# Halving some key chunks on GpSimd, 24 instead of 60 identity products, and a newly searched instruction order in a fused attention and two-MLP kernel

## The chip, the cores and the metric

The kernel runs on one core of one Trainium2 chip. The metric is the device time of one execution in microseconds (us): 1506.7 us, the median of 3 runs (1506.11 to 1508.36). About 0.2%, some 3 us, is what a measurement of this kernel can tell from no change.

## What is computed

Three layers follow each other: an attention whose 768 keys are averages of 16 inputs each, an MLP with a squared ReLU, and an MLP with a rational activation. There are 12,288 tokens of 128 features; both MLPs have 2,048 hidden features.

```python
kv_pool = kv.reshape(B, H // r, r, W // r, r, C).mean(axis=(2, 4))   # r = 4: 16 inputs a key
k = v = kv_pool.reshape(B, -1, C) @ w_sr
s = scale * (q @ k.transpose(0, 2, 1)); a = softmax(s)
x = a @ v
r = np.maximum(x @ w_in, 0.0);  x = (r * r) @ w_out                  # first MLP
h = x @ w2_in
P = a[0] + a[1] * h + a[2] * h**2 + a[3] * h**3
Q = 1.0 + np.abs(b[0]) * np.abs(h) + np.abs(b[1]) * h**2
return (P / (Q + 1e-06)) @ w2_out                                    # second MLP
```

## The kernel before, in words

Tokens go through in 25 blocks: one of 384, 22 of 512, then 384 and 256. All activations lie features-first, so a product has 128 rows and up to 512 columns. To keep float32 accuracy, most products are split into a high and a low part and done as three fast (fp32r) products; the others are plain float32 products, which show as two instructions each. "room" is one large on-chip tensor: it first holds the 16 chunks of key inputs (48 keys of 16 inputs, 384 KB each) and afterwards, as numbered rings of buffers, the values between the stages (tags Z, U, K, g1, aT, e, o, qr).

At the start, `go2` (L480) sums the 16 inputs of each key on VectorE, chunk by chunk. Meanwhile TensorE multiplies an identity with itself (`warm`, L489, 60 times). `go` (L499) then makes the keys of one half from 8 chunks; ScalarE (L503) and VectorE (L507) split them into `k_hi` and `k_lo`; `decode` (L552 to L584) loads the MLP weights, which arrive as 64-bit numbers, and turns them into float32 with four VectorE operations a piece.

For each block there are then, by function:

- `attention`: scores (L671, 24 instructions a block), minimum (L675, VectorE), exponential (L678, ScalarE), the sum's reciprocal (L685, L686), scaling (L689, GpSimd), transposes (L712), their evacuation and split (L716 to L732, ScalarE or VectorE), the product with the values (L741 to L745), and the split of its result, `split` (L771 to L777).
- `mlp1`: `mm3` (L797 to L799) into a PSUM bank, ReLU (L839 on ScalarE or L842 on VectorE), square (L845 on ScalarE or L848 on GpSimd), for 10 of the 16 slices a split (L857, L863), and the output product `mmo` (L811 plain, L815 to L817 split).
- `mlp2`, in 8 groups of two slices: `mm3`; |h| (L936), a square of h (L950) and, for six groups, two GpSimd operations (L939, L941) or, for the other two, one on ScalarE (L944); a logarithm and an exponential (L961, L962); four VectorE operations (L952, L974, L976, L979); for two groups a split (L989 on ScalarE or L990 on VectorE, then L992 on GpSimd); the output product L811.

No loop sets the order in which these stand on each engine. `Plan.order` does, when the program is built: each piece of work is entered with a priority (`off` moves those of one kind), one or several engines it may run on with costs (`c_actp`, `c_dve2`, `c_pool` and so on) and a handicap for each (`rl_act`, `mh_dve`, ...), and the buffers and banks it needs (`bufs`, `caps`). The plan walks through time with these costs and writes out one fixed order for each engine. On the chip every engine takes its instructions strictly in that order. The table SQUARES holds the numbers for this branch of the program; a second table, TERMS, serves coefficients that the first form can't take, and doesn't run here.

Of the kernel before, what the change touches and what calls it, by code (L numbers as in the profile page):

```python
# [10 lines left out]
F32 = mybir.dt.float32  # L11
# [30 lines left out]
    lead1=17.5,  # L42
    leada=18.0,
# [2 lines left out]
    g=2,  # L46
    pair=('kk', 'qp', 'sq2', 'ln', 'y0', 'g0', 'tt', 'rr', 'g2', 'ml', 'mh'),
    rem=[],
    md_act=0.5,
    md_dve=0,  # L50
    rl_act=0,
    rl_dve=2,
    qh_act=0,
    qh_dve=8,
    spd=[],
    spl=[0, 3],
    qpool=[0, 1, 3, 4, 6, 7],
    sq_act=0,
    sq_pool=2,
    gh_act=0.5,  # L60
    gh_dve=60,
    mh_act=1,
    mh_dve=0.5,
    ml_pool=4,
    ml_dve=60,
    ev_dve=4,
    hi_dve=1,
    rg=1,
    low=5,
    avs=5,  # L70
    warm=60,
    head=[384],
    tail=[384, 256],
    off=dict(
        mh2=-197.25, mh1=-120.0, sc=0.25, tr=2.25, nr=-301.75, g2=-55.25, ex=-101.0, kk=-215.75, rl=-4.0,
        tt=68.25, ev=84.5, mo2=13.75, ln=84.25, g0=-20.75, ab=-96.25, sq=142.5, y0=36.0, mn=-267.75, qp=134.25,
        av=-195.25, mo1=5.5, sP=95.25, sq2=146.0, rr=248.75, mh=-48.5, ml=-221.5,
    ),
    free=150.0,
)  # L80
# [5 lines left out]
    lp=0,  # L86
# [282 lines left out]
def program(ctx, tc, CFG, fast, co, room, wsr, qT, kvT, w1_in, w1_out, w2_in, w2_out, outT):  # L369
# [32 lines left out]
    turn, ring_at, at = {}, {}, 0  # L402
    for t in [x for x in RINGS if x not in ("o", "qr")] + ["o", "qr"]:
        at = max(at, NKEY * R2) if t == "o" else at
        ring_at[t] = at
        at += RINGS[t] * bufs[t]
    assert at <= room_size(CFG)
# [46 lines left out]
    for t in RINGS:  # L454
        for n in range(bufs[t]):
            x = ring_at[t] + n * RINGS[t]
            P.hold[t, n] = [("poolT", c) for c in range(0, NKEY, KC) if c * R2 < x + RINGS[t] and x < (c + KC) * R2]
# [7 lines left out]
    def dma(prio, nbytes, emit, new=(), rd=(), wr=()):  # L465
        P.op(prio, (DMA, nbytes / 325.0 + 20.0, emit, 0), new, rd, wr)
# [6 lines left out]
        return go  # L473

    P.op(P0, (POOL, 500.0, lambda: make_identity(nc, ident), 0), new=[("const", "ident")])
    for c in range(0, NKEY, KC):
        def go2(c=c):
            t = mk("o", "pool") if c == 0 else tiles["pool"]
            kv = room[:, c * R2:(c + KC) * R2].rearrange("p (k r) -> p k r", r=R2)
            nc.vector.tensor_reduce(out=t[:, c:c + KC], in_=kv, axis=AX.X, op=ALU.add)  # L480
        dma(P0, KC * R2 * 512, lambda: None, new=[("const", ("kv", c))])
        P.op(P0, (DVE, c_dve(KC * R2), go2, 0), new=[("const", ("poolT", c))] + ([] if c else [("o", "pool")]),
             rd=[("kv", c)] + (["pool"] if c else []))
    dma(P0, sizes[0] * 512, load_q(0), new=[("qr", ("qr", 0))])

    def warm(i):
# [2 lines left out]
            nc.tensor.matmul(out=o[:, 0:128], lhsT=ident, rhs=ident, start=True, stop=True)  # L489
        return go  # L490
    for i in range(CFG["warm"]):
        P.op(1e6, (PE, c_mm4(128), warm(i), 0), new=[("st", "warm")] if i == 0 else [],
             rd=["ident"], wr=["warm"] if i else [])

    for h in range(2):
# [545 lines left out]
            emit()  # L1041


def room_size(cfg):

    n = {t: w * cfg["bufs"][t] for t, w in RINGS.items()}
    return max(sum(n.values()), 768 * 16 + n["o"] + n["qr"])


@with_exitstack  # L1050
def attn_moe_moe(
# [21 lines left out]
    room = pool.tile([128, max(room_size(SQUARES), room_size(TERMS))], F32, name="room")  # L1073
# [105 lines left out]
```

## Time and profile before

| | |
|---|---|
| median of 3 runs | 1506.7 us |
| the profiled execution | 1506.16 us |
| its span, first to last instruction | 1504.3 us |
| busy: TensorE (PE) | 1457.4 us, 97% |
| busy: ScalarE (ACT) | 1413.7 us, 94% |
| busy: VectorE (DVE) | 1388.8 us, 92% |
| busy: GpSimd (POOL) | 1314.7 us, 87% |
| chain that ended last | PE 64%, POOL 13%, ACT 12%, DVE 7%, issue 3% |

The profiled execution takes 1.9 us more than its span, and lies within the range of the runs. PE's busy time is modelled: products overlap in their pipeline, so the distance from one start to the next tells more than a product's duration. A wait is put down to the instruction whose semaphore came last.

### The profile page before, as it was taken

To read this page: it belongs to the slowest core of one execution; us is meant where nothing else is said; L and a number is where in the kernel's file an instruction comes from. 1 tells how busy PE (TensorE), PEld (TensorE's weight loads), DVE (VectorE), ACT (ScalarE), POOL (GpSimd) and SP (SyncE) were. 2 spreads that over 40 slices of the span, in tenths; PEclk is the share of its full clock that TensorE was granted. 3 is DMA by queue.
4 is the path that set the end of the run, shared out by engine and by line. 5 is a ranking of instruction groups with operands and counts; after the bars stand their busy time and mean duration, and the time that the engine had idled before them with its cause. 6 is when DMAs were issued, how large, how long until landed. Compare 5 with 4: busy or idle time off the path is not lost.

```text
span 1504.3 us, 18834 instructions
## 1 busy us (share of the span) xinstructions
PE 1457.4 (97%) x6063; PEld 1057.8 (70%) x6063; DVE 1388.8 (92%) x1848; ACT 1413.7 (94%) x2371; POOL 1314.7 (87%) x995
## 2 busy tenths in 40 slices
PE   6899999999999999999999999999999999999996
PEld 6777767766677677677676776777767667767764
DVE  6998999999999999999999998999988999999997
ACT  1789999999999999999999999999999999999997
POOL 1799998898998998988999889889889989899974
PEclk9999999999999999999999999999999999999998
DMA  7310000000000000000000000000000000000000
GB/s 266 112 50 7 6 8 15 8 8 15 7 8 8 15 4 11 8 8 15 8 8 15 8 8 7 15 8 7 15 7 8 8 11 6 8 5 4 7 8 12
DMA packets 15548, 28.62 MB, mean 19 GB/s; under 512 B 1744, under 2 KB 6736, under 8 KB 15440
## 3 DMA queue, kind: packets, MB, share of 16 engines
q1 hardware_dynamic: 15440, 27.34, 5.4%
q8 instruction: 49, 0.80, 0.2%
q14 instruction: 59, 0.48, 0.1%
HBM read 21.04 MB, written 6.29 MB: 18 GB/s over the span
## 4 chain that ended last, share of the span: by engine, by line
PE 64%; POOL 13%; ACT 12%; DVE 7%; issue 3%; DMA 0%; POOLq 0%; SPq 0%; ACTq 0%; DVEq 0%
PE psum L811 16%; PE psum L797 8%; PE psum L798 8%; PE psum L799 8%; PE psum L671 5%; POOL room L941 4%; PE psum L815 3%; PE psum L816 3%; PE psum L817 3%; PE psum L712 3%; POOL gL L863 2%; POOL room L939 2%; ACT room L950 2%; ACT room L961 2%; ACT room L936 2%
## 5 line engine op out<-in xcount | busy, mean ns | idle before, releaser
L941 POOL TENSOR_TENSOR room<-room 128x1024 f32<-128x1024 f32 (+2 forms) x150 | 347.3, 2316 | 3.0
L863 POOL TENSOR_TENSOR gL<-room,gH 128x512 fp32r<-128x512 f32 (+2 forms) x250 | 311.9, 1260 | 8.9 <-PE psum L816 2.6
L952 DVE SCALAR_TENSOR_TENSOR room<-room,cf,psum 128x512 f32<-128x512 f32 (+2 forms) x400 | 281.0, 719 | 16.5 <-ACT room L950 14.4
L811 PE MATMUL psum<-room,w1o 128*128 128x512 f32 (+2 forms) x600 | 288.8, 587 | 4.4 <-DVE room L979 4.4
L974 DVE SCALAR_TENSOR_TENSOR room<-room,v,psum 128x1024 f32<-128x1024 f32 (+2 forms) x200 | 246.3, 1233 | 29.7 <-ACT psum L962 27.8
L950 ACT ACTIVATE room<-psum,cf 128x512 f32<-128x512 f32 (+2 forms) x400 | 271.9, 709 | 0.0
L848 POOL TENSOR_TENSOR room<-room 128x512 f32<-128x512 f32 (+2 forms) x220 | 222.0, 1021 | 30.3 <-ACT room L839 19.0
L976 DVE SCALAR_TENSOR_TENSOR psum<-room,cf,psum 128x1024 f32<-128x1024 f32 (+2 forms) x200 | 247.3, 1237 | 0.0
L961 ACT ACTIVATE room<-room,cf 128x1024 f32<-128x1024 f32 (+2 forms) x200 | 229.2, 1148 | 17.9 <-POOL room L941 17.0
L979 DVE SCALAR_TENSOR_TENSOR room<-psum,room 128x1024 f32<-128x1024 f32 (+2 forms) x200 | 235.0, 1175 | 2.9
L936 ACT ACTIVATE room<-psum 128x512 f32<-128x512 f32 (+2 forms) x400 | 228.5, 608 | 6.1 <-PE psum L799 4.3
L939 POOL TENSOR_SCALAR room<-room,cf 128x1024 f32<-128x1024 f32 (+2 forms) x150 | 163.8, 1092 | 69.0 <-ACT room L936 57.2
L962 ACT ACTIVATE psum<-room 128x1024 f32<-128x1024 f32 (+2 forms) x200 | 206.0, 1031 | 4.1 <-DVE room L979 3.2
L797 PE MATMUL psum<-xh,w0h 128*128 128x512 f32 (+2 forms) x400 | 186.6, 466 | 4.2 <-ACT room L1012 1.5
L797 PE MATMUL psum<-yh,w1h 128*128 128x512 f32 (+2 forms) x400 | 185.5, 464 | 5.0 <-DVE room L952 1.3
L839 ACT ACTIVATE room<-psum 128x512 f32<-128x512 f32 (+2 forms) x272 | 161.6, 619 | 3.5 <-PE psum L799 3.1
L811 PEld LDWEIGHTS psum<-room,w1o 128*128 128x128 f32 x600 | 112.8, 193 | 66.5 <-issue 40.5
L857 ACT ACTIVATE gH<-room 128x512 fp32r<-128x512 f32 (+2 forms) x250 | 156.2, 659 | 0.7 <-POOL room L848 0.4
L799 PE MATMUL psum<-yh,w1l 128*128 128x512 f32 (+2 forms) x400 | 154.1, 385 | 0.0
L798 PE MATMUL psum<-yl,w1h 128*128 128x512 f32 (+2 forms) x400 | 153.8, 385 | 0.0
L798 PE MATMUL psum<-xl,w0h 128*128 128x512 f32 (+2 forms) x400 | 153.5, 384 | 0.2 <-DVE xl L777 0.2
L799 PE MATMUL psum<-xh,w0l 128*128 128x512 f32 (+2 forms) x400 | 153.5, 384 | 0.0
(126 smaller groups left out, 3196.4 us busy)
## 6 DMA issues: line engine op xcount, KB each, us to landing
room<-in_kv_dram SPq DMA_DIRECT2D x16, 384.0 KB, 7.8
room<-in_q_dram SPq DMA_DIRECT2D x22, 256.0 KB, 2.6
out_dram<-room SPq DMA_DIRECT2D x22, 256.0 KB, 2.0
room<-in_moe_w_in_dram SPq DMA_DIRECT2D x8, 512.0 KB, 3.9
room<-in_moe_w_out_dram SPq DMA_DIRECT2D x16, 256.0 KB, 2.7
room<-in_q_dram SPq DMA_DIRECT2D x2, 192.0 KB, 5.4
out_dram<-room SPq DMA_DIRECT2D x2, 192.0 KB, 1.9
room<-in_q_dram SPq DMA_DIRECT2D x1, 128.0 KB, 2.1
```

The source lines that it names most:

```text
L797: nc.tensor.matmul(out=out, lhsT=w_hi[m][:, sl], rhs=hi, start=True, stop=False)
L798: nc.tensor.matmul(out=out, lhsT=w_hi[m][:, sl], rhs=lo, start=False, stop=False)
L799: nc.tensor.matmul(out=out, lhsT=w_lo[m][:, sl], rhs=hi, start=False, stop=True)
L811: nc.tensor.matmul(out=o, lhsT=w_o[m][:, place[m][fi], :], rhs=rhs(), start=first, stop=last)
L863: nc.gpsimd.tensor_tensor(out=mk("gL", gl)[:, :T], in0=G(), in1=f(tiles[gh][:, :T]), op=ALU.subtract)
L936: one("ab", ACT, c_actp, lambda v: act(out=v(uu), in_=v(hh), func=AF.Abs), "U", [hh])
L941: one("qp", POOL, c_pool, lambda v: nc.gpsimd.tensor_tensor(out=v(ku), in0=v(ku), in1=v(uu), op=ALU.mult), None, [uu], [ku])
L950: one("sP", ACT, ptr(c_actp), lambda v: act(out=v(zz), in_=v(hh), func=AF.Square, bias=co["c"]), "Z", [hh])
L952: one("z3", DVE, ptr(c_dve), lambda v: stt(out=v(zz), in0=v(zz), scalar=co["nd"], in1=v(hh), op0=ALU.subtract, op1=ALU.mult), None, [hh], ...
L961: one("ln", ACT, ptr(c_acts), lambda v: act(out=v(uu), in_=v(ku), func=AF.Ln, bias=dl_ap), None, [ku], [uu])
L974: one("g0", DVE, ptr(c_dve), lambda v: stt(out=v(zz), in0=v(zz), scalar=e0, in1=v(yy), op0=ALU.add, op1=ALU.mult), None, [yy], [zz])
L976: one("tt", DVE, c_dl, lambda v: stt(out=v(yy), in0=v(ku), scalar=dl, in1=v(yy), op0=ALU.add, op1=ALU.mult), None, [ku], [yy])
```

## The change

Three things are done. On the 7 even chunks among the first 14, GpSimd adds the upper 8 inputs of each key to the lower 8 in place, and VectorE then sums 8 values instead of 16. The identity products go from 60 to 24. And nearly every number of the table SQUARES is new (handicaps, offsets, ring sizes, bank caps), as are some costs that the plan uses, so that the order on every engine is new from the start to the end. `places` also gives each ring buffer a place of its own, buffer by buffer, which says for which key chunk it must wait.

```diff
-    lp=1,
+    lp=0,
-        qr=1, qh=1, ql=1, e=4, mn=14, sm=16, aT=1, xh=1, xl=1, yh=2, yl=2, aH=2, aL=2, g1=8, U=2, K=4, Z=7, o=1,
+        qr=1, qh=1, ql=1, e=4, mn=17, sm=21, aT=1, xh=2, xl=1, yh=2, yl=2, aH=3, aL=2, g1=8, U=2, K=3, Z=7, o=1,
...
-        h2=3, yb=6, sc=6, st=6, x=1, h1=5, y1=1, y2=1, dc=1,
+        h2=6, yb=5, sc=6, st=6, x=1, h1=5, y1=1, y2=1, dc=1,
...
-    sq_act=0,
-    sq_pool=2,
+    sq_act=8,
+    sq_pool=0.5,
...
-    warm=60,
+    warm=24,
...
-    return (66 + n / 2) / 0.96 + 61 * ptr + 300
+    return (66 + n / 2) / 0.96 + 61 * ptr + 700
...
+    def half(c):
+
+        return c // KC % 2 == 0 and c < NKEY - 2 * KC
     for c in range(0, NKEY, KC):
         def go2(c=c):
             t = mk("o", "pool") if c == 0 else tiles["pool"]
             kv = room[:, c * R2:(c + KC) * R2].rearrange("p (k r) -> p k r", r=R2)
+            if half(c):
+                kv = kv[:, :, 0:R2 // 2]
             nc.vector.tensor_reduce(out=t[:, c:c + KC], in_=kv, axis=AX.X, op=ALU.add)
...
+        def add2(c=c):
+            kv = room[:, c * R2:(c + KC) * R2].rearrange("p (k r) -> p k r", r=R2)
+            nc.gpsimd.tensor_tensor(out=kv[:, :, 0:R2 // 2], in0=kv[:, :, 0:R2 // 2], in1=kv[:, :, R2 // 2:], op=ALU.add)
...
+        if half(c):
+            P.op(P0, (POOL, c_pool(KC * R2 // 2), add2, 0), wr=[("kv", c)])
...
```

Counted over the whole executed branch, the new order moves these between engines (instructions before, after). Squares: ScalarE 180, 139 (L845), GpSimd 220, 261 (L848). ReLUs: ScalarE 272, 255 (L839), VectorE 128, 145 (L842). High parts of the second MLP: ScalarE 32, 26 (L989), VectorE 18, 24 (L990). Low parts in the attention: GpSimd 25, 0 (L728), VectorE 100, 125 (L732), and 25 copies that fed the GpSimd form (L716, L719) are gone. New: 7 additions on GpSimd. TensorE does the same work but for 36 identity products.

The new file is longer: what stood at L489, L499, L507, L566 stands at L497, L507, L515, L574 now, and L848, L863, L939, L941 are L856, L871, L947, L949.

The first place is the start on TensorE, from the identity products (L489, then L497) to the first scores. Before:

```order
L489 MATMUL psum<-ident 128x128 x57
L499 MATMUL psum<-room,wsr 128x384
L514 MATMUL psum<-wsr,room 128x128 x3
L489 MATMUL psum<-ident 128x128 x3
L499 MATMUL psum<-room,wsr 128x384
L514 MATMUL psum<-wsr,room 128x128 x3
L671 MATMUL psum<-k_hi,qh 128x384 x2
```

In the changed kernel:

```order
L497 MATMUL psum<-ident 128x128 x24
L507 MATMUL psum<-room,wsr 128x384
L522 MATMUL psum<-wsr,room 128x128 x3
L507 MATMUL psum<-room,wsr 128x384
L522 MATMUL psum<-wsr,room 128x128 x3
L679 MATMUL psum<-k_hi,qh 128x384 x2
```

The first key product stood behind 57 identity products and stands behind 24 now; the second has none ahead of it any more.

The second place is the same stretch on VectorE, from the sums of the key inputs (L480, then L482) to the low part of the second half of the keys (the second L507, then L515). Before:

```order
L480 TENSOR_REDUCE room<-room 128x48 x10
L507 SCALAR_TENSOR_TENSOR k_lo<-psum,k_hi 128x384
L480 TENSOR_REDUCE room<-room 128x48
L529 SCALAR_TENSOR_TENSOR v_lo<-psum,v_hi 128x384
L480 TENSOR_REDUCE room<-room 128x48 x5
L566 TENSOR_SCALAR psum<-room 128x512
L574 SCALAR_TENSOR_TENSOR psum<-room,psum 128x512
L507 SCALAR_TENSOR_TENSOR k_lo<-psum,k_hi 128x384
```

In the changed kernel:

```order
L482 TENSOR_REDUCE room<-room 128x48 x12
L515 SCALAR_TENSOR_TENSOR k_lo<-psum,k_hi 128x384
L482 TENSOR_REDUCE room<-room 128x48 x4
L537 SCALAR_TENSOR_TENSOR v_lo<-psum,v_hi 128x384
L574 TENSOR_SCALAR psum<-room 128x512
L582 SCALAR_TENSOR_TENSOR psum<-room,psum 128x512
L587 SCALAR_TENSOR_TENSOR psum<-room,psum 128x512
L515 SCALAR_TENSOR_TENSOR k_lo<-psum,k_hi 128x384
```

Two more sums stand ahead of the first low part, and three weight operations instead of two ahead of the second.

The third place is GpSimd in the middle of the run, from the low part of one block's queries (ql, the 13th) on. Before:

```order
L650 TENSOR_TENSOR ql<-room,qh 128x512
L689 TENSOR_SCALAR room<-room,sm 128x768
L863 TENSOR_TENSOR gL<-room,gH 128x512
L939 TENSOR_SCALAR room<-room,cf 128x1024
L848 TENSOR_TENSOR room<-room 128x512
L728 TENSOR_TENSOR aL<-room,aH 128x512
L941 TENSOR_TENSOR room<-room 128x1024
L863 TENSOR_TENSOR gL<-room,gH 128x512 x3
```

In the changed kernel:

```order
L658 TENSOR_TENSOR ql<-room,qh 128x512
L697 TENSOR_SCALAR room<-room,sm 128x768
L856 TENSOR_TENSOR room<-room 128x512
L697 TENSOR_SCALAR room<-room,sm 128x768
L856 TENSOR_TENSOR room<-room 128x512
L947 TENSOR_SCALAR room<-room,cf 128x1024
L856 TENSOR_TENSOR room<-room 128x512
L949 TENSOR_TENSOR room<-room 128x1024
```

The attention's low part (L728) is gone from the queue, and three squares (L856) stand where one stood, two of them ahead of the first of the second MLP's products (L947) and one between it and its second half (L949).

## Rows read from the trace of the kernel before

**Rows 1.** The page: busy time of each engine over the whole span.

```profile
PE 1457.4 (97%) x6063; PEld 1057.8 (70%) x6063; DVE 1388.8 (92%) x1848; ACT 1413.7 (94%) x2371; POOL 1314.7 (87%) x995
```

**Rows 2.** Busy time by stretch: us, each engine's busy us (instructions), granted clock, DMA.

```profile
50.00:100.00 50.00, 49.05 (x259) 42.41 (x258) 48.16 (x106) 44.97 (x99) 45.02 (x48) 1.00 0.33 105
60.00:1440.00 1380.00, 1368.69 (x5629) 985.40 (x5628) 1289.83 (x1661) 1339.79 (x2219) 1261.66 (x942) 1.00 0.04 12
1450.00:1500.00 50.00, 38.59 (x148) 27.09 (x146) 45.14 (x70) 41.08 (x85) 26.34 (x23) 0.83 0.02 5
```

**Rows 3.** Timeline of the start: start us, length us, instruction, idle time before it.

```profile
8.13 14.77 PE L489 MATMUL psum<-ident 128*128 128x128 f32 x114 [8.13 <-POOL ident masks.py:199]
9.20 8.69 DVE L480 TENSOR_REDUCE room<-room 128x48 f32<-128x768 f32 x10 [0.65 <-DVE cf L1089]
...
22.73 0.81 PE L499 MATMUL psum<-room,wsr 128*128 128x384 f32 x2
...
24.17 0.56 DVE L507 SCALAR_TENSOR_TENSOR k_lo<-psum,k_hi 128x384 fp32r<-128x384 f32 x1 [6.28 <-ACT k_hi L503]
...
30.40 1.65 PE L499 MATMUL psum<-room,wsr 128*128 128x384 f32 x2 [5.52 <-DVE room L480]
...
32.61 0.56 DVE L507 SCALAR_TENSOR_TENSOR k_lo<-psum,k_hi 128x384 fp32r<-128x384 f32 x1 [0.93 <-ACT k_hi L503]
```

**Rows 4.** Line L1083, the 16 loads of key inputs: first and last issue, landing.

```profile
L1083 SPq DMA_DIRECT2D room<-in_kv_dram x16: 327/416/646, 2.1 to 14.0; - x16
...
DMA to landing us min/median/max: 4.6/7.8/8.2
```

**Rows 5.** Timeline, issue of the first weight loads on the DMA queue.

```profile
16.01 2.27 SPq L552 DMA_DIRECT2D room<-in_moe_w_in_dram  x3
```

**Rows 6.** Busy time by stretch around the second key product, granted clock after the engines.

```profile
28.00:30.00 2.00, 0.00 (x0) 0.00 (x0) 2.00 (x3) 0.00 (x0) 0.03 (x1) 0.74 1.04 336
32.00:34.00 2.00, 2.00 (x10) 2.00 (x9) 1.21 (x3) 1.04 (x3) 0.00 (x0) 0.50 0.15 52
```

**Rows 7.** Timeline of the DMA queue: two of the blocks' stores, 17 blocks apart.

```profile
225.53 0.34 SPq L1016 DMA_DIRECT2D out_dram<-room  x1
...
1239.68 0.34 SPq L1016 DMA_DIRECT2D out_dram<-room  x1
```

**Rows 8.** The chain that ended last: start us, length us, what; PE's pace.

```profile
654.89 1.41 PE psum L671 x8
656.30 0.23 PE psum L797
...
659.03 0.23 PE psum L815
...
661.93 3.43 PE psum L811 x8
...
801.80 1.21 PE psum L712 x11
```

**Rows 9.** Groups by line and shape: count, busy us, mean ns, idle before.

```profile
L848 POOL TENSOR_TENSOR room<-room 128x512 f32<-128x512 f32 x196 | 204.2, 1055 | 27.4 <-ACT room L839 17.2 <-DVE room L842 4.7 <-DVE sm L685 2.5
...
L845 ACT ACTIVATE room<-room 128x512 f32<-128x512 f32 x156 | 99.0, 664 | 0.9 <-DVE room L842 0.6
...
L732 DVE TENSOR_TENSOR aL<-psum,aH 128x512 fp32r<-128x512 f32 x88 | 59.5, 684 | 2.3 <-ACT aH L722 1.7
...
L989 ACT ACTIVATE mH<-room 128x1024 fp32r<-128x1024 f32 x27 | 29.5, 1092 | 0.0
...
L728 POOL TENSOR_TENSOR aL<-room,aH 128x512 fp32r<-128x512 f32 x22 | 28.3, 1288 | 0.5
...
L990 DVE CAST mH<-room 128x1024 fp32r<-128x1024 f32 x17 | 23.9, 1406 | 0.8 <-PE psum L817 0.6
```

**Rows 10.** Waits, 60 to 1440 us: total us, times, longest us.

```profile
PE psum L797 <- ACT room L678: 2.5, 4, 1.3
...
ACT room L961 <- POOL room L941: 13.5, 32, 1.2
```

More of the change, by code (lines that the diff above doesn't have):

```diff
@@ L48 @@
     rem=[],
-    md_act=0.5,
-    md_dve=0,
-    rl_act=0,
+    md_act=1,
+    md_dve=60,
+    rl_act=8,
     rl_dve=2,
-    qh_act=0,
-    qh_dve=8,
+    qh_act=4,
+    qh_dve=1,
     spd=[],
     spl=[0, 3],
-    qpool=[0, 1, 3, 4, 6, 7],
-    sq_act=0,
-    sq_pool=2,
+    qpool=[0, 1, 3, 4, 5, 7],
+    sq_act=8,
+    sq_pool=0.5,
     gh_act=0.5,
     gh_dve=60,
-    mh_act=1,
-    mh_dve=0.5,
-    ml_pool=4,
+    mh_act=8,
+    mh_dve=0,
+    ml_pool=0,
     ml_dve=60,
-    ev_dve=4,
-    hi_dve=1,
+    ev_dve=8,
+    hi_dve=0,
     rg=1,
-    low=5,
+    low=4,
     avs=5,
-    warm=60,
+    warm=24,
     head=[384],
@@ L400, in program @@
     tiles = {}
[L402 to L407, printed above, removed]
+    turn = {}
+    place_of, extra = places(CFG, None if fast else room_size(SQUARES))
+    more = const.tile([128, extra], F32, name="more") if extra else None
     def mk(tag, key, shape=None, dtype=None):
@@ L414, in mk @@
             n = turn[tag] = turn.get(tag, -1) + 1
-            at = ring_at[tag] + n % bufs[tag] * RINGS[tag]
-            t = room[:, at:at + RINGS[tag]]
+            in_room, at = place_of[tag, n % bufs[tag]]
+            t = (room if in_room else more)[:, at:at + RINGS[tag]]
             if dtype:
@@ L453, in program @@
     P = Plan(CFG)
[L454 to L457, printed above, removed]
+    for (t, n), (in_room, x) in place_of.items():
+        P.hold[t, n] = [("poolT", c) for c in range(0, NKEY, KC)
+                        if in_room and c * R2 < x + RINGS[t] and x < (c + KC) * R2]
     def f(t):
@@ L479, in go2 @@
             kv = room[:, c * R2:(c + KC) * R2].rearrange("p (k r) -> p k r", r=R2)
+            if half(c):
+                kv = kv[:, :, 0:R2 // 2]
             nc.vector.tensor_reduce(out=t[:, c:c + KC], in_=kv, axis=AX.X, op=ALU.add)
-        dma(P0, KC * R2 * 512, lambda: None, new=[("const", ("kv", c))])
-        P.op(P0, (DVE, c_dve(KC * R2), go2, 0), new=[("const", ("poolT", c))] + ([] if c else [("o", "pool")]),
-             rd=[("kv", c)] + (["pool"] if c else []))
+        def add2(c=c):
+            kv = room[:, c * R2:(c + KC) * R2].rearrange("p (k r) -> p k r", r=R2)
+            nc.gpsimd.tensor_tensor(out=kv[:, :, 0:R2 // 2], in0=kv[:, :, 0:R2 // 2], in1=kv[:, :, R2 // 2:], op=ALU.add)
+        P.op(P0, (DMA, KC * R2 * 512 / 520.0, lambda: None, 0), new=[("const", ("kv", c))])
+        if half(c):
+            P.op(P0, (POOL, c_pool(KC * R2 // 2), add2, 0), wr=[("kv", c)])
+        P.op(P0, (DVE, c_dve(KC * R2 // (2 if half(c) else 1)), go2, 0),
+             new=[("const", ("poolT", c))] + ([] if c else [("o", "pool")]), rd=[("kv", c)] + (["pool"] if c else []))
     dma(P0, sizes[0] * 512, load_q(0), new=[("qr", ("qr", 0))])
@@ L491, in program @@
     for i in range(CFG["warm"]):
-        P.op(1e6, (PE, c_mm4(128), warm(i), 0), new=[("st", "warm")] if i == 0 else [],
+        P.op(1e6, (PE, 260.0, warm(i), 0), new=[("st", "warm")] if i == 0 else [],
              rd=["ident"], wr=["warm"] if i else [])
@@ L1041, in program, with places @@
             emit()
+def places(cfg, size):
+    bufs, at, out = cfg["bufs"], 768 * 16, {}
+    for t in ("o", "qr"):
+        for n in range(bufs[t]):
+            out[t, n] = (True, at)
+            at += RINGS[t]
+    low, extra = 0, 0
+    for t in RINGS:
+        for n in range(0 if t in ("o", "qr") else bufs[t]):
+            w = RINGS[t]
+            if low + w <= 768 * 16:
+                out[t, n], low = (True, low), low + w
+            elif size is None or at + w <= size:
+                out[t, n], at = (True, at), at + w
+            else:
+                out[t, n], extra = (False, extra), extra + w
+    return (out, extra) if size is not None else (out, 0)
 def room_size(cfg):
-    n = {t: w * cfg["bufs"][t] for t, w in RINGS.items()}
-    return max(sum(n.values()), 768 * 16 + n["o"] + n["qr"])
+    return max(x + RINGS[t] for (t, n), (_, x) in places(cfg, None)[0].items())
 @with_exitstack
@@ L1072, in attn_moe_moe @@
     wsr = pool.tile([128, w_sr.shape[1]], F32, name="wsr")
[L1073 removed]
+    room = pool.tile([128, room_size(SQUARES)], F32, name="room")
     col = lambda n, name: pool.tile([128, n], F32, name=name)
```

12 lines of the change are left out of this document (6 added, 6 removed).

## The prediction

> **What bounds the kernel now.** I read the page first: TensorE is busy 97% of the span, ScalarE 94%, VectorE 92%, GpSimd 87% [rows 1]. Four nearly full engines say little by a mean, so I cut the run into start, middle and end. In the middle, 1380 us, ScalarE is busy for 1339.8 us (97.1%), VectorE for 93.5%, GpSimd for 91.4%; in the 50 us before the end TensorE is busy for 38.6 us only, VectorE for 45.1 us [rows 2].
>
> How much TensorE waits in the middle is seen in its pace. Two stores 17 blocks apart give (1239.68 - 225.53) / 17 = 59.66 us a block [rows 7]. Where TensorE runs without a gap, 12 fp32r products of 512 columns take 2.73 us (0.2275 each), 8 score products 1.41 us (0.176), 8 halves of plain products 3.43 us (0.857 a whole one), 11 transposes 1.21 us (0.11) [rows 8]. A block has 153, 24, 19 and 24 of them: 34.8 + 4.2 + 16.3 + 2.6 = 57.9 us. So TensorE is the bound, and 59.66 - 57.9 = 1.76 us a block is lost waiting, some 40 us over the 23 blocks of the middle. No order can save more than that there.
>
> In the start I read the timeline. The identity products run from 8.13 us; the first key product starts at 22.73 us, directly behind them [rows 3]. Its data was there sooner: VectorE did 10 sums in 8.69 us from 9.20 us on, so the eighth was done at 16.2 us. VectorE then had a low part (L507) next, which needs that key product, and sat idle 6.28 us for it until 24.17 us with six sums still to do. So the second key product waited for the last sum until 30.40 us [rows 3]. The identity products thus held up VectorE, and VectorE the keys.
>
> **The start, step by step.** Removing 36 of 60 identity products: at the mean pace of the 57 that stood first, (22.73 - 8.13) / 57 = 0.256 us, 24 end near 14.3 us, before the eighth sum. The first key product then goes at about 16.3 us, and the idle 6.28 us are gone. What is late next is the data: the 16 chunk loads are issued until 14.0 us and land 7.8 us later, 8.2 at most [rows 4]. The last chunk is there at about 22 us, its full sum (8.69 / 10 = 0.87 us) ends at 23.0. The second key product moves from 30.40 to about 23.0: 7.4 us.
>
> Not all of it arrives at the scores. Behind the sums VectorE now has three weight operations, not two, ahead of the second low part. They need the first weights, issued at 16.01 us [rows 5] behind the key chunks, and so hardly there before 24 to 25 us. I have no row for one of them alone; a sum of 768 inputs at 0.87 us is the nearest long one, and 0.684 us for a 512-wide VectorE operation [rows 9] is the nearest in size. I take the latter: 25.2 + 3 x 0.684 = 27.3 us, so the low part is at 27.3 us where it was at 32.61 [rows 3]. I take **5.5 us** as gained. The ends are 0 (the lead is lost again until about 60 us, as the weights arrive no sooner) and 8 (all of it stays, and the shorter sums help).
>
> The 7 additions on GpSimd: a GpSimd operation of 512 pairs takes 1.055 us [rows 9], one of 384 is bounded by that and by 384/512 of it, 0.79. There is one addition for every two chunks, and chunks are issued 11.9 / 15 = 0.79 us apart [rows 4], so GpSimd, which has no other work there, keeps up. They spare VectorE at most 7 x 0.87 / 2 = 3.0 us of sums. As the data sets the end of the sums, I cost and credit them nothing; without that cover the range of the term holds them.
>
> Fewer identity products also mean a cooler start. After its idle time the clock fell: 0.74 at 28 to 30 us, 0.50 (1.2 GHz) at 32 to 34 us [rows 6]. With the key products at 16.3 and 23.0 us the idle time between is about 5.5 us, as long as now, so I expect the same fall 7 us earlier, and no cost. If the low clock lasted 4 us of TensorE work longer, that would cost 2 us; the range of the term holds it.
>
> **The middle, step by step.** ScalarE loses 36 full-width squares at 0.664 us (23.9 us) and 5 high parts at 1.092 us (5.5 us) [rows 9]. Its other full-width forms net to two instructions less (1.3 us), and narrower ones take off perhaps 4 us: **35 us** less. GpSimd takes the 36 squares at 1.055 us (+38.0) and drops 22 low parts at 1.288 us (-28.3) [rows 9]: 10 us more. VectorE takes 5 high parts at 1.406 us (+7.0), and its 0.684 us forms net to two more (L732 +22, L842 +12, L725 -16, L719 -11, L774 -5) [rows 9]: about 9 us more.
>
> So ScalarE's idle time in the middle goes from 40 to some 75 us, GpSimd's from 118 to 108, VectorE's from 90 to 81 [rows 2]. What TensorE waits for there is small in each place. The view of its waits lists 15 pairs with 11.3 us in all, the largest on the exponential L678 with 2.5 us [rows 10]; the pairs that end on ScalarE make 6.0 us of it, just over half. I charge half of the 40 us lost to ScalarE and let it shrink as ScalarE's idle time grows, 20 x (1 - 40/75) = 9 us. The other half grows with the lost idle time of the two others, about a tenth of 20, so 2 us, which leaves a gain of 7. A regular order can give a little more, since what is lost are short waits in places that the new order treats anew; I take **8 us**. Ends: all 40 us gained, which no row supports with three engines above 90%, and a loss, the rival below.
>
> **The end** has the same VectorE operations on its last two blocks, in nearly the same order, and VectorE is its busiest engine [rows 2]. I cost it at 0, with 2 us either way.
>
> **The sum.** Against the profiled execution, 1506.16 us (0.5 us under the median of the runs): 1506.2 - 5.5 - 8 = **1492.7 us**.
>
> A rule against the change: the Trainium skill, in GPSIMD Engine Reference, section 4.1, advises VectorE and not GpSimd for elementwise products, since two-input operations run about twice as long there. The same square indeed takes 1.055 us on GpSimd and 0.664 us on ScalarE here [rows 9]. By the rule the moved squares are a bad trade, and the sum would be that of the slower rival below; by the rows they buy time on the fuller engine.
>
> **Rivals.**
>
> *Only the start gains.* TensorE's 1.76 us a block comes from bursts, in which the order of a few instructions matters and not an engine's mean. Then a lighter ScalarE changes nothing: 1506.2 - 5.5 = 1500.7 us. For it: no single wait of TensorE's is long [rows 10]. Against it: ScalarE has only 40 us idle in 1380.
>
> *The middle gains much more.* Half of the 40 us go, as all four queues get shorter: 1506.2 - 5.5 - 20 = 1480.7 us. For it: the order is new everywhere. Against it: VectorE and GpSimd get more work.
>
> *Nothing is left.* The start's lead is lost while the weights are loaded, since VectorE is busy for 48.2 of the 50 us after 50 us [rows 2], and the middle stays: 1506 us.
>
> *Slower, by GpSimd's queue.* The added squares stand between the two GpSimd operations of the second MLP (L939, L941), and ScalarE's logarithm waits for L941 already, 32 times, 13.5 us in all, up to 1.2 us [rows 10]. If a square delays that chain as far as TensorE, it costs its 1.055 us; all 41 would cost 43 us. Without a gain in the middle, slower by over 0.2% is reached when a fifth of them do, (5.5 + 3) / 43. With 27% it is 11.6 us: 1506.2 - 5.5 + 11.6 = 1512.3 us. Against it: GpSimd has 118 us idle in the middle, and lost 22 longer operations from its queue.
>
> That the change doesn't do what it says is excluded by the order: 24 identity products, 7 additions and 41 squares moved all stand there.
>
> **How the numbers follow.** The forecast gets 0.45 (its own range 1485 to 1499), only the start 0.17, the large gain 0.15, nothing left 0.12, slower 0.11. About 0.2%, 3 us, is what a measurement can tell from no change. Faster by more: 0.45 + 0.17 + 0.15 = 0.77; within it 0.12; slower 0.11. The range 1479 to 1507 takes in the first four cases nearly whole and leaves out the slower one and the outer part of the large gain, under 0.2.
>
> **What would show it.** In the new profile the first key product should start near 16 us and the second near 23 us, with no idle time of 6 us on VectorE between. ScalarE's busy time should be about 35 us lower, GpSimd's 10 to 17 higher. The distance of 17 stores should give 59.2 to 59.5 us a block. I am wrong if the second key product moves and the scores do not, if the blocks stay at 59.66 us, or if TensorE's waits now end on GpSimd lines.

## The result, and the profile after

The changed kernel takes 1487.57 us (median of 4 runs, 1486.91 to 1488.9) against 1507.48 us for the kernel before beside it: a ratio of 0.987, 95% interval 0.9853 to 0.9887, so 19.6 us less. It lies in the range given, on the side given most, and 5 us under the predicted 1492.7 us. The profiled execution takes 1486.91 us, its span 1484.7 us where 1504.3 us stood.

Busy times on the page of the changed kernel:

```profile
PE 1439.5 (97%) x5991; PEld 1053.8 (71%) x5991; DVE 1386.9 (93%) x1857; ACT 1393.4 (94%) x2318; POOL 1334.1 (90%) x1021
```

Against [rows 1], ScalarE is 20.3 us less busy (35 were expected), GpSimd 19.4 more (10 to 17), VectorE 1.9 less (9 more). ScalarE and GpSimd moved the way that was forecast, by other amounts; VectorE moved the other way.

The start in the timeline of the changed kernel, TensorE and VectorE (start us, length us, instruction, idle time before it):

```profile
8.23 7.63 PE L497 MATMUL psum<-ident 128*128 128x128 f32 x48 [8.23 <-POOL ident masks.py:199]
...
10.01 5.50 DVE L482 TENSOR_REDUCE room<-room 128x48 f32<-128x384 f32 x8 [0.68 <-issue]
...
15.69 0.81 PE L507 MATMUL psum<-room,wsr 128*128 128x384 f32 x2
...
19.95 3.13 DVE L482 TENSOR_REDUCE room<-room 128x48 f32<-128x768 f32 x4
...
23.14 1.65 PE L507 MATMUL psum<-room,wsr 128*128 128x384 f32 x2 [5.97 <-DVE room L482]
23.70 0.70 DVE L574 TENSOR_SCALAR psum<-room 128x512 int32<-128x512 int32 x1 [0.16 <-DMA room<-in_moe_w_in_dram]
...
25.72 0.78 PE L679 MATMUL psum<-k_hi,qh 128*128 128x384 f32 x2
25.77 0.55 DVE L515 SCALAR_TENSOR_TENSOR k_lo<-psum,k_hi 128x384 fp32r<-128x384 f32 x1
```

The key products start at 15.69 and 23.14 us (forecast 16.3 and 23.0), the second low part at 25.77 us where it was at 32.61 [rows 3]: 6.8 us sooner, not 5.3 (27.3). The step that was too long is the wait for the first weights: they were there at 23.70 us, not 25.2. VectorE's idle time of 6.28 us is gone; TensorE's stop ahead of the second key product, 5.97 us, stays, as forecast. So does the clock's fall:

```profile
22.00:24.00 2.00, 0.86 (x2) 0.56 (x3) 1.84 (x4) 0.74 (x2) 0.97 (x1) 0.50 1.01 401
...
26.00:28.00 2.00, 2.00 (x13) 1.98 (x12) 2.00 (x5) 1.55 (x4) 0.00 (x0) 0.97 0.96 321
```

These are windows of the changed kernel, the granted clock behind the engines' busy times: 0.50 (1.2 GHz) at 22 to 24 us, after TensorE had stood for 5.97 us, and 0.97 in the window 4 us on. As before, a second fall follows it.

In the middle, busy time of the changed kernel from 60 to 1420 us:

```profile
60.00:1420.00 1360.00, 1351.47 (x5579) 981.80 (x5579) 1279.40 (x1648) 1311.95 (x2150) 1262.61 (x945) 1.00 0.03 11
```

and of the kernel before:

```profile
60.00:1420.00 1360.00, 1348.69 (x5539) 971.38 (x5538) 1270.68 (x1639) 1320.34 (x2179) 1242.37 (x922) 1.00 0.04 12
```

In the same 1360 us TensorE starts 40 more products. At 1351.47 / 5579 = 0.242 us each that is 10 us of work, an estimate, as products differ in length. The first 60 us, before:

```profile
0.00:60.00 60.00, 40.72 (x239) 37.77 (x240) 45.16 (x108) 22.40 (x48) 19.15 (x25) 0.91 0.55 193
```

and in the changed kernel:

```profile
0.00:60.00 60.00, 40.61 (x212) 36.03 (x213) 51.34 (x127) 30.07 (x65) 33.75 (x42) 0.89 0.64 222
```

Without the identity products (120 and 48 instructions) these are 119 and 164, so the changed kernel is 45 products ahead at 60 us and 85 at 1420 us. By the same 0.242 us the 85 are 20.6 us, as much as the whole gain: the end adds nothing that this estimate can tell. The second key product starts 7.3 us sooner, so some 12 of the 19.6 us are gained in the middle.

The stores, which were to show the pace, mislead:

```profile
237.88 0.34 SPq L1024 DMA_DIRECT2D out_dram<-room  x1
...
1213.73 0.34 SPq L1024 DMA_DIRECT2D out_dram<-room  x1
```

(1213.73 - 237.88) / 17 = 57.40 us a block where [rows 7] gave 59.66, less even than the 57.9 us of TensorE's unbroken work in the prediction. The new order finishes blocks at other points of its run; the distance of two stores is no pace then.

Waits, 60 to 1420 us (total us, times, longest us), of the kernel before: ScalarE's longest, then three of TensorE's, PEld being the weight load ahead of a product:

```profile
ACT room L961 <- POOL room L941: 12.9, 31, 1.2
...
PEld psum L797 <- DVE room L952: 14.0, 35, 1.2
PEld psum L797 <- ACT room L839: 12.6, 28, 1.3
PEld psum L797 <- ACT room L678: 8.7, 14, 1.8
```

and of the changed kernel, with the largest wait of a product itself (PE) as the last:

```profile
ACT room L969 <- POOL room L949: 20.8, 38, 1.7
...
PEld psum L805 <- DVE room L960: 11.2, 32, 1.2
...
PEld psum L805 <- ACT room L686: 5.3, 8, 1.2
...
PEld psum L805 <- ACT room L847: 3.5, 12, 0.4
...
PE psum L824 <- POOL mL L1000: 1.8, 4, 0.8
```

Summed over all of the view's pairs, products and loads that wait for ScalarE go from 42.8 to 22.7 us, for VectorE from 54.6 to 48.3, for GpSimd from 13.0 to 10.1. (Loads run ahead of products, so these us are not all lost; they show where TensorE is held.) The prediction would have been wrong if TensorE's waits now ended on GpSimd: the largest wait of a product does (L1000, 1.8 us), but GpSimd's sum is still the smallest of the three. The logarithm's wait for GpSimd grew from 12.9 us to 20.8, as the slower rival had it. TensorE's loads (L797, now L805) don't wait longer for the last VectorE operation behind that chain: 6.1 us for L979 before, 4.7 for L987 now.

### The profile page after: what moved, and what is told of

It is laid out like the page before. It is cut to its first block, busy times and chain, and to the rows that moved or that the text cites. A ratio compares the mean times of both kernels' runs of the same rounds, so it can differ in the third digit from the quotient of the medians.

```text
span 1484.7 us, 18746 instructions
## 1 busy us (share of the span) xinstructions
PE 1439.5 (97%) x5991; PEld 1053.8 (71%) x5991; DVE 1386.9 (93%) x1857; ACT 1393.4 (94%) x2318; POOL 1334.1 (90%) x1021
## 4 chain that ended last, share of the span: by engine, by line
PE 67%; POOL 13%; ACT 8%; DVE 7%; issue 3%; DMA 1%; SPq 0%; POOLq 0%; ACTq 0%; DVEq 0%
PE psum L819 17%; PE psum L805 9%; PE psum L806 8%; PE psum L807 8%; PE psum L679 4%; PE psum L824 4%; POOL room L949 4%; PE psum L825 4%; PE psum L823 4%; PE psum L720 4%; POOL gL L871 3%; POOL room L947 2%; POOL room L856 2%; PE psum L750 1%; PE psum L749 1%
## 5 line engine op out<-in xcount | busy, mean ns | idle before, releaser
L949 POOL TENSOR_TENSOR room<-room 128x1024 f32<-128x1024 f32 (+2 forms) x150 | 348.3, 2322 | 3.6
L871 POOL TENSOR_TENSOR gL<-room,gH 128x512 fp32r<-128x512 f32 (+2 forms) x250 | 313.0, 1262 | 20.8 <-PE psum L824 15.8
L819 PE MATMUL psum<-room,w1o 128*128 128x512 f32 (+2 forms) x600 | 285.2, 583 | 4.0 <-DVE room L987 4.0
L856 POOL TENSOR_TENSOR room<-room 128x512 f32<-128x512 f32 (+2 forms) x261 | 262.3, 1022 | 12.5 <-ACT room L847 6.6
L982 DVE SCALAR_TENSOR_TENSOR room<-room,v,psum 128x1024 f32<-128x1024 f32 (+2 forms) x200 | 246.1, 1232 | 21.2 <-ACT psum L970 19.4
L958 ACT ACTIVATE room<-psum,cf 128x512 f32<-128x512 f32 (+2 forms) x400 | 262.8, 688 | 0.0
L987 DVE SCALAR_TENSOR_TENSOR room<-psum,room 128x1024 f32<-128x1024 f32 (+2 forms) x200 | 235.2, 1177 | 3.1
L944 ACT ACTIVATE room<-psum 128x512 f32<-128x512 f32 (+2 forms) x400 | 223.4, 593 | 12.5 <-PE psum L807 6.5
L947 POOL TENSOR_SCALAR room<-room,cf 128x1024 f32<-128x1024 f32 (+2 forms) x150 | 164.7, 1098 | 48.3 <-ACT room L944 36.0
L970 ACT ACTIVATE psum<-room 128x1024 f32<-128x1024 f32 (+2 forms) x200 | 202.7, 1015 | 0.7 <-DVE room L960 0.3
L805 PE MATMUL psum<-yh,w1h 128*128 128x512 f32 (+2 forms) x400 | 191.2, 478 | 4.8 <-DVE room L987 3.5
L805 PE MATMUL psum<-xh,w0h 128*128 128x512 f32 (+2 forms) x400 | 182.8, 457 | 1.6 <-DVE xh L782 1.2
L847 ACT ACTIVATE room<-psum 128x512 f32<-128x512 f32 (+2 forms) x255 | 148.3, 601 | 5.1 <-PE psum L807 3.2
L865 ACT ACTIVATE gH<-room 128x512 fp32r<-128x512 f32 (+2 forms) x250 | 149.8, 632 | 2.9 <-POOL room L856 2.6
```

What stands on the lines that cost most here:

```text
L805: nc.tensor.matmul(out=out, lhsT=w_hi[m][:, sl], rhs=hi, start=True, stop=False)
L819: nc.tensor.matmul(out=o, lhsT=w_o[m][:, place[m][fi], :], rhs=rhs(), start=first, stop=last)
L856: nc.gpsimd.tensor_tensor(out=G(), in0=G(), in1=G(), op=ALU.mult)
L871: nc.gpsimd.tensor_tensor(out=mk("gL", gl)[:, :T], in0=G(), in1=f(tiles[gh][:, :T]), op=ALU.subtract)
L949: one("qp", POOL, c_pool, lambda v: nc.gpsimd.tensor_tensor(out=v(ku), in0=v(ku), in1=v(uu), op=ALU.mult), None, [uu], [ku])
L958: one("sP", ACT, ptr(c_actp), lambda v: act(out=v(zz), in_=v(hh), func=AF.Square, bias=co["c"]), "Z", [hh])
```

## The experiments

Two theories stood at first. **Load:** the middle gains since work left ScalarE, the fullest helper. **Order:** it gains since the order searched happens to have fewer places where TensorE is held, whatever the engines' loads. Differences from the kernel before are (ratio - 1) x 1507.5 us, each against runs of the kernel before beside it; the intervals are about 2.5 us either way (1.5 us for a3, b1 and n1, with more runs).

### The start: identity products, additions

Two edits of the kernel before keep its order. The first issues 24 of 60 identity products; the second adds the additions and half sums to that:

```diff
+            if i < 24:
                 nc.tensor.matmul(out=o[:, 0:128], lhsT=ident, rhs=ident, start=True, stop=True)
```
```diff
             kv = room[:, c * R2:(c + KC) * R2].rearrange("p (k r) -> p k r", r=R2)
+            if c // KC % 2 == 0 and c < NKEY - 2 * KC:
+                nc.gpsimd.tensor_tensor(out=kv[:, :, 0:R2 // 2], in0=kv[:, :, 0:R2 // 2], in1=kv[:, :, R2 // 2:], op=ALU.add)
+                kv = kv[:, :, 0:R2 // 2]
```

Two edits of the changed kernel undo parts and keep the new order: full sums without additions (the addition's line is taken out too), and, beyond that, 60 identity products, all of them ahead of the first key product.

```diff
-            if half(c):
-                kv = kv[:, :, 0:R2 // 2]
```
```diff
+            for _ in range(37 if i == 0 else 1):
                 nc.tensor.matmul(out=o[:, 0:128], lhsT=ident, rhs=ident, start=True, stop=True)
```

> The kernel before with its own order, in which only the first 24 of the 60 identity products are issued. Theory (the start's gain is the identity products alone and lasts to the end): the second key product moves from 30.4 us to about 23.5 us and the time falls by 6 to 8 us against before. Rival (the start's lead is lost again while the weights are loaded): the key product moves and the time stays within 1.5 us of before.

> As the run with 24 identity products, with the seven GpSimd additions and the shorter sums on VectorE as well, order otherwise that of before. Theory (the last chunk's arrival ends the sums): within 1 us of the run with 24 identity products alone. Rival (VectorE's sums end the start): 2 to 3 us faster than that run.

> The changed kernel with its order, without the seven additions, so that VectorE sums all 16 inputs of every key. Theory (arrival ends the sums): 0 to 1 us slower than the changed kernel. Rival (the additions carry part of the gain): 2 to 4 us slower.

> The changed kernel's order with the old start: 60 identity products ahead of the first key product and no additions, so only the new order from there on is left of the change. Theory (start about 7 us, middle about 12): 5 to 7 us slower than the changed kernel, some 13 us faster than before. Rival (all of the gain is the middle): within 1.5 us of the changed kernel.

| run | us | ratio (95%) | against before |
|---|---|---|---|
| before, 24 identity products | 1500.99 | 0.9953 (0.9937 to 0.997) | -7.1 |
| the same, with additions | 1499.84 | 0.995 (0.9934 to 0.9967) | -7.5 |
| after, without additions | 1488.44 | 0.9869 (0.9852 to 0.9885) | -19.7 |
| after, 60 identity products, no additions | 1493.74 | 0.9901 (0.9885 to 0.9918) | -14.9 |

The first three come out as their theories had it, within what can be measured. The fourth gains some 2 us more against before than expected, and its distance from the changed kernel, 4.7 us, lies just under the range. The timeline of TensorE in the first of them:

```profile
16.29 0.91 PE L500 MATMUL psum<-room,wsr 128*128 128x384 f32 x2 [1.05 <-DVE room L480]
...
24.09 1.65 PE L500 MATMUL psum<-room,wsr 128*128 128x384 f32 x2 [6.23 <-DVE room L480]
```

in the third:

```profile
23.72 1.65 PE L505 MATMUL psum<-room,wsr 128*128 128x384 f32 x2 [5.80 <-DVE room L480]
```

and in the last:

```profile
23.75 0.81 PE L506 MATMUL psum<-room,wsr 128*128 128x384 f32 x2
...
29.23 1.41 PE L506 MATMUL psum<-room,wsr 128*128 128x384 f32 x2 [4.01 <-DVE room L480]
```

Both orders show the same thing: 36 products fewer in the queue let the first key product go on its data, and the second key product goes 6.3 us sooner (30.40 to 24.09) in the old order, 5.5 us (29.23 to 23.72) in the new, both without additions. In the total that is 7.1 us in the old order and 19.6 - 14.9 = 4.7 us in the new. The additions bring the second key product forward by another 0.6 us in the new order (23.72 to 23.14), and are worth nothing in the total that can be measured in either. So with the old start the middle and the end gain about 15 us by themselves; by the changed kernel's own trace, above, it is 12. The forecast was 8.

### What a us of added work costs, engine by engine

If load is the cause, then giving load back must cost what taking it away gained. Into the changed kernel went unread extra operations of 480 columns, two a block behind first products (L805): on ScalarE 46 squares, on VectorE 46 sums, on GpSimd 35 squares (every second one left out at one of the two places). Two of the three went into the kernel before too.

```diff
             mm3(mk("h1", h)[:, :T], 0, fi, "x", b)
+            if fast and 1 <= b <= 23 and fi in (3, 11):
+                nc.scalar.activation(out=spare, in_=f(w_hi[0][:, 0:480]), func=AF.Square)
```

> The changed kernel with 46 additional squares of 480 columns on ScalarE that nobody reads, two in each of 23 blocks, some 29 us of work: about the work that the change took off ScalarE. Theory (the middle gains because ScalarE is less full): 7 to 12 us slower than the changed kernel. Rival (the middle gains by the new order as such): 0 to 3 us slower.

> The changed kernel with 46 additional sums of 480 columns on VectorE that nobody reads, at the same places, some 27 us of work. Theory (ScalarE is the engine whose time counts): clearly less than what the work on ScalarE costs, 3 to 6 us. Rival (all engines are so full that any work counts the same, or VectorE the more, as it is now at 94%): as much as on ScalarE or more.

> The changed kernel with 35 additional squares of 480 columns on GpSimd that nobody reads, at the same places, some 35 us of work. Theory: 2 to 6 us slower, since GpSimd still idles for 100 us in the middle. Rival (GpSimd's queue is what TensorE waits for now): over 10 us slower.

> The kernel before with the same 35 additional squares on GpSimd, at the same places as in the run on the changed kernel, where they cost 21 us. Theory (the new order stands a delay on GpSimd better than the old): 26 us or more. Rival (both orders stand it alike): 17 to 25 us.

> The kernel before with the same 46 additional squares on ScalarE, at the same places as in the run on the changed kernel, where they cost 9 us. Theory (ScalarE was fuller before, so that work on it cost more): 13 us or more. Rival (work on ScalarE costs the same in both orders): 6 to 12 us.

Their durations in the view of the tile "spare" (ns, min/median/max, first and last start us), in the first run:

```profile
L847 ACT ACTIVATE spare<-w0h x46: 587/614/801, 76.4 to 1383.8; 128x480 f32<-128x480 f32 x46
```

in the second:

```profile
L847 DVE TENSOR_REDUCE spare<-w0h x46: 633/646/655, 76.8 to 1382.7; 128x1 f32<-128x480 f32 x46
```

in the third:

```profile
L847 POOL TENSOR_TENSOR spare<-w0h x35: 977/989/1535, 77.2 to 1399.2; 128x480 f32<-128x480 f32 x35
```

Count times median is the work added; the cost is the difference from the same kernel without it. By the expectations, ScalarE in the changed kernel came out as the theory had it (8.0 us), VectorE, GpSimd and GpSimd in the kernel before as the rivals had it, and ScalarE in the kernel before between the two.

| added to | engine | work added, us | run, us | ratio (95%) | cost, us | cost per us |
|---|---|---|---|---|---|---|
| after | ScalarE | 28.2 | 1496.68 | 0.9923 (0.9907 to 0.994) | 8.0 | 0.28 |
| after | VectorE | 29.7 | 1495.76 | 0.9921 (0.9905 to 0.9938) | 7.7 | 0.26 |
| after | GpSimd | 34.6 | 1508.69 | 1.0005 (0.9995 to 1.0015) | 20.4 | 0.59 |
| before | GpSimd | 34.5 | 1531.67 | 1.0156 (1.0139 to 1.0173) | 23.5 | 0.68 |
| before | ScalarE | 28.2 | 1520.95 | 1.0083 (1.0066 to 1.0099) | 12.5 | 0.44 |

The engine with most idle time has the highest price. ScalarE's operations overlap: its busy time rose by 19.9 and 22.2 us only, VectorE's by 23.8, GpSimd's by 31.5 and 34.7. Per us of busy time the prices are 0.40 and 0.56, 0.32, 0.65 and 0.68, each uncertain by about 0.1; GpSimd's stays the highest. The prices, with GpSimd's against the gain, are too small to carry the middle. Put against the counted moves of the prediction: ScalarE 35 us less at 0.28 to 0.44 gains 10 to 15 us; GpSimd 10 us more at 0.59 to 0.68 costs 6 to 7; VectorE 9 us more at 0.26 costs 2. That leaves a gain of 1 to 7 us of the 12 to 15. With the measured busy times and the prices per busy us it is less: 20.3 us off ScalarE gain 8 to 11, 12.5 on GpSimd (19.4 less the 6.9 of the additions at the start) cost 8, 1.9 off VectorE gain 0.6, together 0 to 4 us. (The prices hold for work at these two places of a block; taking them for the moved work is an estimate.) That the new order stands mishaps better was a third idea: 20.4 against 23.5 us says no within the uncertainty, 8.0 against 12.5 says a little.

### Two of the moves without the new order

In the kernel before, 40 of ScalarE's 180 squares go to GpSimd in place, at the point where ScalarE would have had them; everything else stands as it was.

```diff
         def sq_a():
+            moved["n"] = moved.get("n", 0) + 1
+            if moved["n"] % 9 in (2, 6):
+                return sq_p()
             nc.scalar.activation(out=G(), in_=G(), func=AF.Square)
```

> The kernel before with its own order, in which 40 of the 180 squares on ScalarE are done on GpSimd, each at the point of the program where it stood. Theory (a lighter ScalarE is what gains): 4 to 9 us faster than before. Rival (the gain is in the order; a square moved without a new order only delays GpSimd's queue): same as before or up to 15 us slower.

It takes 1536.07 us, 1.0189 (1.0172 to 1.0206), 28.5 us more than before. Its waits, 60 to 1420 us:

```profile
ACT room L964 <- POOL room L944: 33.7, 53, 1.6
ACT gH L860 <- POOL room L851: 15.0, 16, 2.4
...
PE psum L797 <- DVE room L955: 5.6, 9, 1.4
```

That is 13 us beyond even the rival's range. The pair of logarithm and second GpSimd product goes from 12.9 to 33.7 us, ScalarE's split (L860) now waits 15.0 us for GpSimd's squares, and VectorE's L955 now stops TensorE's products for 5.6 us (1.0 us for the same operation, L952, before), where [rows 10] had 2.5 us as the largest pair of a product. Here is the mechanism of the prediction's slower rival, at work: 0.7 us for each moved square. The changed kernel moves about as many squares and doesn't pay this. What spares it wasn't tried by itself; it puts the squares, and all the rest, elsewhere.

The other part of the change on GpSimd is that 25 low parts of the attention left it. In the kernel before, they go to VectorE in place:

```diff
             def lo3_p(aT=aT):
-                nc.gpsimd.tensor_tensor(
+                nc.vector.tensor_tensor(
```

> The kernel before with its own order, in which the 25 low parts of the attention that GpSimd makes (L728) are made on VectorE from the same copy, each at its old point of the program: GpSimd loses 32 us of work that TensorE soon needs, VectorE gains about 17 us. Theory (GpSimd's queue is what the middle is short of, and the change relieved it of this urgent work): 8 to 15 us faster than before, most of what the new order gains in the middle. Rival (the gain lies in where everything stands, not in this move): within 3 us of before.

It takes 1512.79 us, 1.0031 (1.0021 to 1.0041), 4.7 us more, which neither the theory nor the rival had. Its group by line and shape:

```profile
L728 DVE TENSOR_TENSOR aL<-room,aH 128x512 fp32r<-128x512 f32 x22 | 21.7, 986 | 0.9 <-ACT room L716 0.9
```

and one of its waits, 60 to 1420 us:

```profile
POOL room L939 <- ACT room L936: 63.3, 36, 5.9
```

GpSimd becomes 21 us lighter (1293.5 us busy) and waits longer for ScalarE (63.3 us; 50.7 in the kernel before, over the same window). So the low parts' leaving GpSimd doesn't gain by itself, either. It isn't quite the changed kernel's move: that one reads the low part's input from PSUM (684 ns, [rows 9]) and drops the 25 copies, which this run keeps. By the prices GpSimd's 21 us x 0.68 should have gained 14 us, less 16 us x 0.26 = 4 for VectorE (1405.2 us busy). A price found by adding work doesn't hold for taking work away in place, which makes the 0 to 7 us above a rough estimate.

### A neighbour of the new order

Last, one number of the table was changed, the time that the plan lets pass between a buffer's last use and its next (150 to 140 ns of the plan's clock). The plan then writes out another order from about a fourteenth of the run on, with the same start.

```diff
-    free=150.0,
+    free=140.0,
```

> The changed kernel with one number of its table changed that costs nothing on the chip (the plan takes a buffer as free 140 ns after its last use, not 150), so that the planner lays out another order from a fourteenth of the run on, with the same start: 24 instructions fewer on ScalarE, 28 more on VectorE, 4 fewer on GpSimd. Theory (the gain hangs on the particular order that was searched for): 5 to 20 us slower than the changed kernel. Rival (the gain lies in the table's handicaps, ring sizes and split between the engines, which any order of this table keeps): within 3 us.

It takes 1507.12 us, 0.9994 (0.9984 to 1.0004): 18.7 us more than the changed kernel, and level with the kernel before. Its busy times:

```profile
PE 1450.1 (96%) x5991; PEld 1055.2 (70%) x5991; DVE 1398.3 (93%) x1885; ACT 1393.7 (93%) x2294; POOL 1325.3 (88%) x1017
```

ScalarE has the changed kernel's load to 0.3 us, GpSimd less, VectorE 11 us more; at 0.26 that is 3 us. These loads don't make the other 15. Where the order loses, its windows show:

```profile
225.00:250.00 25.00, 20.17 (x67) 13.06 (x66) 22.43 (x29) 20.20 (x34) 23.47 (x20) 0.80 0.07 22
237.00:242.00 5.00, 2.39 (x12) 1.75 (x10) 3.73 (x7) 4.40 (x6) 5.00 (x4) 0.76 0.18 52
242.00:247.00 5.00, 2.78 (x5) 1.56 (x6) 5.00 (x5) 3.93 (x8) 5.00 (x5) 0.50 0.00 0
...
300.00:325.00 25.00, 22.01 (x83) 14.82 (x82) 23.08 (x31) 24.12 (x39) 24.45 (x18) 0.93 0.04 12
...
325.00:1420.00 1095.00, 1087.15 (x4425) 780.03 (x4425) 1030.63 (x1298) 1048.07 (x1674) 1002.25 (x739) 1.00 0.03 9
```

In the first 25 us TensorE starts 67 products, the changed kernel 102; in the 25 us from 300 us on 83, the changed kernel 94. The timeline of its GpSimd queue in the first of them:

```profile
234.56 1.30 POOL L871 TENSOR_TENSOR gL<-room,gH 128x512 fp32r<-128x512 f32 x1
235.82 1.04 POOL L856 TENSOR_TENSOR room<-room 128x512 f32<-128x512 f32 x1
236.82 1.27 POOL L658 TENSOR_TENSOR ql<-room,qh 128x512 fp32r<-128x512 f32 x1
238.07 1.34 POOL L697 TENSOR_SCALAR room<-room,sm 128x768 f32<-128x768 f32 x1
```

and of its TensorE:

```profile
236.14 0.39 PE L823 MATMUL psum<-gH,w0oh 128*128 128x512 f32 x1
...
236.83 0.49 PE L720 MATMUL psum<-ident,room 128*128 128x128 f32 x3
239.46 2.08 PE L720 MATMUL psum<-ident,room 128*128 128x128 f32 x9 [2.15 <-POOL room L697]
242.75 0.79 PE L823 MATMUL psum<-gH,w0oh 128*128 128x512 f32 x1 [1.21 <-ACT gH L865]
245.01 0.80 PE L824 MATMUL psum<-gL,w0oh 128*128 128x512 f32 x1 [1.47 <-POOL gL L871]
```

The softmax's scaling (L697) stands in GpSimd's queue behind a low part, a square and the queries' low part, so it ends at 239.41 us. TensorE's transposes wait 2.15 us for it, the clock falls to 0.50 (1.2 GHz) in 242 to 247 us, and the next products take 0.79 us where the one ahead took 0.39, and wait again, the second for another low part of GpSimd's (L871). GpSimd is busy for all of these 10 us, in a run in which it has nothing to do for a tenth of the time.

From 325 us to 1420 us, the kernel before and the changed kernel:

```profile
325.00:1420.00 1095.00, 1086.84 (x4414) 776.03 (x4413) 1021.78 (x1271) 1065.90 (x1731) 994.97 (x726) 1.00 0.03 9
...
325.00:1420.00 1095.00, 1088.86 (x4460) 784.88 (x4459) 1030.88 (x1286) 1062.92 (x1722) 1017.77 (x751) 1.00 0.03 9
```

So the neighbour loses in two ways. In the two windows of 25 us it starts 46 products fewer than the changed kernel, by 0.242 us each some 11 of the 18.7 us, in jams at which the clock falls (0.80 and 0.93 there); neither the kernel before nor the changed kernel has such a fall in the middle (1.00 over 60 to 1420 us). From 325 us on it starts 11 products more than the kernel before, where the changed kernel starts 46 more. Its level total is therefore no proof that the changed kernel's gain hangs on its one order. What is shown is that another order of nearly this table, with the same ring sizes and bank caps, loses as much as the whole change gained, and that where no clock falls it has about a quarter of the changed kernel's lead over the kernel before (11 of 46 products).

## Why the prediction was right, and where not

- **The start** (5.5 us forecast): shown, 4.7 us in the new order, 7.1 in the old. The step on the first weights (25.2 us, from issue order alone) was 1.5 us late, and its own sum gives 32.61 - 27.3 = 5.3 us and not 5.5. That the second key product goes at 23.14 us, so near the forecast's 23.0, owes 0.6 us to the additions, which the forecast left out: with full sums it goes at 23.72 us, and at 24.09 us in the old order, as the sums end later than one sum behind the last chunk.
- **The additions at nothing:** shown for the total, both ways round (0.4 and 0.1 us, each known to 2 or 3 us). The reason given, that the arrival of the data sets the end, holds only in part, by the 0.6 us above. VectorE's 16 sums in the changed kernel (ns, min/median/max):

```profile
L482 DVE TENSOR_REDUCE room<-room x16: 541/943/953, 10.0 to 22.1; 128x48 f32<-128x768 f32 x9, 128x48 f32<-128x384 f32 x7
```

  A half sum takes 0.54 us, a full one 0.94. An addition takes 0.99 us, inside the 0.79 to 1.055 given, and from the third on the trace has it wait for its chunk.
- **The clock at nothing:** the same two falls, a little longer. In windows of 10 us the granted clock was 0.95, 0.71 and 0.83 from 20 us on before, and 0.96, 0.69 and 0.66 from 10 us on now; what is missing to full clock sums to 5.1 and 6.9 us, partly over idle time. The 1.8 us lie within the 2 us given as the term's end.
- **The middle** (8 us forecast, 12 to 15 measured): the sign was right, the size and the reason were not. The step that failed is "let it shrink as ScalarE's idle time grows", with the two others' terms beside it. The ScalarE term of 9 us is near what the prices give (8 to 15), and the waits for ScalarE did halve. But GpSimd's added 10 us were put at a part of 2 us where its price asks 6 to 8; together the loads carry 0 to 7 us by these estimates, and moved in place, without a new order, the squares lose 28.5. That the sum still came out within its range is luck in this term: its reason can't carry it. What carries the rest is left to the order, by exclusion: the neighbour, with nearly the same loads, gives the gain back, over half of it in jams that the kernel before doesn't have either. The rival of the large gain had this reason ("the order is new everywhere"), and the remark on bursts, made for the start alone, was nearer than the forecast's.
- **What the middle's term was worked out from:** half of the loss was charged to ScalarE because it ends over half of TensorE's waits. That view had the products alone, whose pairs sum to 10.3 us (the 11.3 given is TensorE's idle time). With the weight loads, VectorE ends the most, 54.6 us against ScalarE's 42.8 before. And the 40 us lost came from the distance of two stores, which is no pace: the changed kernel's 57.40 us a block lie under the 57.9 that TensorE was to need without a gap.
- **Busy times:** VectorE came out 2 us less and not 9 more, as the duration of one form changed with the order (below), which counts times old means can't see. ScalarE lost 20 us and not 35, in part because its operations overlap: in the chain of the kernel before, three squares in a row take 1.56 us, 0.52 each, where the mean duration is 0.664 [rows 9].

```profile
92.42 1.56 ACT room L845 x3
```

- **The slower rival:** its mechanism exists at its price (28.5 us for 40 squares; the changed kernel's longer waits of the logarithm for L949), but the changed kernel doesn't pay it.

Open: why the new order gains in the middle, which is argued from what the loads can't carry and not shown by itself. Ring sizes, bank caps and single handicaps weren't tried alone in the old order, and of the neighbours only one ran; how often one is as good as the changed kernel is not known. No version run here beats the changed kernel: the one without additions is level with it.

## What to carry to other kernels

Where four engines run above 90% in fixed orders, a move between engines is not priced by busy shares; add a known amount of unread work to each engine and see what it costs, take that price as a rough one, and hold the order while testing a move. Treat a searched order as fitted: here one number beside it was worth as much as the whole change, so keep it, look in the trace of a slower one for the stretch in which it loses, and search again after each edit. And look first at what stands in an in-order queue ahead of the first useful instruction: 36 warm-up products fewer were the one part whose gain could be read from the trace beforehand.

## What was not expected of the hardware

- GpSimd, the least busy of the four (87 to 90%), charges 0.59 to 0.68 us for a us of added work, ScalarE and VectorE 0.26 to 0.44 (at the two places tried, in these two orders).
- One jam in GpSimd's queue cost TensorE more than its waits of 2.15, 1.21 and 1.47 us: the clock fell to 0.50 for the products that came next, which took 0.79 us instead of 0.39.
- The low part on VectorE takes 684 ns with one input from PSUM [rows 9] and 986 ns with both from SBUF (the run with the low parts on VectorE; the longest 2748 ns). The Trainium skill (SBUF — State Buffer, Who interferes with whom) says that a VectorE operation with two SBUF inputs contends with a GpSimd operation that reads there, and that a reduction never does. The runs agree: the 46 sums of the second added-work run took 633 to 655 ns, however busy GpSimd was.
- The same cast on VectorE takes 1406 ns in the mean before [rows 9] and 980 after, with 22 of them in place of 17 and another order around them:

```profile
L998 DVE CAST mH<-room 128x1024 fp32r<-128x1024 f32 x22 | 21.6, 980 | 0.9 <-PE psum L825 0.4
```

  A duration read from one order is no constant of the instruction, and that is why VectorE's 22 casts took less in all (21.6 us) than 17 did (23.9 us).
